# Half-width output tiles for the attention matmuls of a fused attention, spectral and gated-MLP kernel, with the key transposes moved ahead of the scores

## The chip, the core and the metric

The kernel runs on one core of one Trainium2 chip. The metric is the device time of one execution in microseconds; less is better. In the profile, PE is TensorE, PEld is its weight load (every matmul first loads its stationary operand), DVE is VectorE, ACT is ScalarE, POOL is GpSimd, and SP is the engine that issues the DMAs.

## What is computed

Three stages follow each other, in float32:

```
# 1. attention, 4 batches x 8 heads, 768 steps, head size 48
state = alpha[:, :, t, :, None] * state + einsum('bhd,bhe->bhde', k[:, :, t], v[:, :, t])
y[:, :, t] = einsum('bhd,bhde->bhe', q[:, :, t], state)
# 2. spectral mixing
theta = x @ w_theta
u = x + w_tok_r @ (x * cos(theta)) + w_tok_i @ (x * sin(theta))
x = u + relu(u @ w_ch)
# 3. gated MLP
h = relu(x @ w_in); out = (h * sigmoid(conv3(h, conv_w))) @ w_out
```

## The kernel before

Attention is done in chunks of 128 steps: 6 chunks per batch, 24 in all, numbered `ci`, with `c = ci % 6` the place in the batch. Heads go in four pairs `p` of two heads `j`; the 48 rows of a head's q and k lie at partitions 0 to 47 (j = 0) or 64 to 111 (j = 1), the partitions between them hold zeros. `a_prep` scales q and k by running products of alpha (DVE). `a_score` makes the 8 score matmuls `sc` (48 rows contracted, so two heads of a pair use different rows of the array), copies them to `pt` (ACT), masks `pt` (POOL), and then makes the 4 key transposes `kps`, copied to `kt` (ACT).

`a_y` makes the output `y` of a chunk: for each head a value matmul (stationary `pt`, 128 columns; moving `v_t`, 48 columns), and for c > 0 for each pair a state matmul (stationary q, 128 columns; moving the state `S`, 96 columns), four value and state groups one after another. ACT copies `y` to `x`. For c < 5 the state update `kv` follows: 4 matmuls (stationary `kt`, 112 columns; moving `v_t`, 96 columns), added to the state by DVE and scaled by POOL (line 293) into the other state buffer. `a_xt` transposes `x` (`xps`), `a_theta` makes `th`, and `m_mix` makes the token mixing `yps` of the batch before. All matmul operands of attention are plain float32; each such matmul stands in the trace as two records of a load and a matmul, called two passes below. The `yps`, `th`, `cps`, `hps` and `ops` matmuls use another float32 type, one pass each.

`a_att(b, c)` gives the order of the code: loads for chunk ci + 2, preparation and scores of chunk ci + 1, then `y`, state update and transposes of chunk ci. A scheduler in the framework then orders the instructions of each engine by its own estimate of times; so the order on an engine is that of the built program. PSUM tiles of attention come from one pool `ps_a` of 5 buffers; `kt` has one buffer, `pt` two.

Of the kernel before, what the change touches and what calls it, by code (L numbers as in the profile page):

```python
# [8 lines left out]
F32 = mybir.dt.float32  # L9
# [9 lines left out]
P = 128  # L19
B, H, S, D = 4, 8, 768, 48  # L20
DM = H * D
DFF = 1024
NP = H // 2
NC = S // P
# [19 lines left out]
def tile_gated_linear_attention__then__spectral_moe__then__conv_gate(  # L44
# [14 lines left out]
    nc = tc.nc  # L59
    NCH = B * NC  # L60

    def mm(o, lhsT, rhs, start, stop):
        nc.tensor.matmul(o, lhsT, rhs, start=start, stop=stop, skip_group_check=True)  # L63
# [34 lines left out]
    def body(top, slow):  # L98
# [4 lines left out]
        ident = const.tile([P, P], F32, name="ident")  # L103
# [35 lines left out]
        with ExitStack() as ph1:  # L139
# [26 lines left out]
            def apool(name, bufs, **kw):  # L166
                return att_ctx.enter_context(tc.tile_pool(name=name, bufs=bufs, **kw))
# [7 lines left out]
            ps_a = apool("ps_a", 5, space=PSUM)  # L175
# [62 lines left out]

            def a_score(ci):
                qh, kh, ftot, vt = prep[ci]  # L240
                scs = [ps_a.tile([P, NP, P], F32, tag="a", name="sc") for _ in range(2)]
                for p in range(NP):
                    for j in range(2):
                        r = slice(64 * j, 64 * j + D)
                        mm(scs[j][:, p, :], kh[r, p, :], qh[r, p, :], True, True)
                pts = []
                for j in range(2):
                    pt = att.tile([P, NP, P], F32, tag="pt", name="pt")
                    marks["pt"] = nc.scalar.copy(pt, scs[j])  # L249
                    nc.gpsimd.affine_select(pt, pt, [[0, NP], [1, P]], ALU.is_ge, 0.0, base=0, channel_multiplier=-1)  # L250
                    pts.append(pt)
                kt = None
                if ci % NC < NC - 1:
                    kps = ps_a.tile([P, 4, P], F32, tag="a", name="kps")
                    for p in range(NP):
                        nc.tensor.transpose(kps[:, p, :], kh[:, p, :], ident)  # L256
                    kt = att.tile([P, 4, P], F32, tag="kt", name="kt", bufs=1)
                    marks["kt"] = nc.scalar.copy(kt, kps)
                scored[ci] = (pts, kt)

            def a_y(ci):
                qh, kh, ftot, vt = prep.pop(ci)
                pts, kt = scored.pop(ci)
                c = ci % NC
                Sp, Sn = Sst[ci % 2], Sst[(ci + 1) % 2]
                y = ps_a.tile([P, DM], F32, tag="a", name="y")
                first = True
                for p in range(NP):
                    for j in range(2):
                        h = 2 * p + j  # L270
                        mm(y[:, h * D : (h + 1) * D], pts[j][:, p, :], vt[:, h * D : (h + 1) * D], first, c == 0)
                        first = False
                    if c > 0:
                        mm(y[:, p * 96 : p * 96 + 96], qh[:, p, :], Sp[:, p, :], False, True)
                x = x_p.tile([P, DM], F32, tag="x", name="x")
                marks["x"] = nc.scalar.copy(x, y)
                xs[ci] = x
                if c < NC - 1:
                    kv = ps_a.tile([P, NP, 2 * D], F32, tag="a", name="kv")
                    for p in range(NP):  # L280
                        mm(kv[:112, p, :], kt[:, p, :112], vt[:, p * 96 : p * 96 + 96], p == 0, True)
                    nft = prep[ci + 1][2]
                    if c > 0:
                        tt = att.tile([P, NP, 2 * D], F32, tag="tst", name="tst", bufs=1)
                        nc.vector.tensor_tensor(tt[:112], Sp[:112], kv[:112], ALU.add)
                    else:
                        tt = Sn
                        for j in range(2):
                            r = slice(64 * j, 64 * j + D)
                            nc.scalar.copy(Sn[r, :, j * D : (j + 1) * D], kv[r, :, j * D : (j + 1) * D])  # L290
                    for j in range(2):
                        r = slice(64 * j, 64 * j + D)
                        nc.gpsimd.tensor_tensor(  # L293
                            Sn[r, :, j * D : (j + 1) * D],
                            tt[r, :, j * D : (j + 1) * D],
                            nft[r].unsqueeze(2).to_broadcast([D, NP, D]),
                            ALU.mult,
                        )
# [66 lines left out]
            def a_att(b, c):  # L365
                ci = b * NC + c
                if slow:
                    xs[ci] = x_p.tile([P, DM], F32, tag="x", name="x")
                    nc.sync.dma_start(out=xs[ci], in_=x_dram[b, c * P : (c + 1) * P, :])
                    a_xt(ci)  # L370
                    return
                if ci + 2 < NCH:
                    a_load(ci + 2)
                if ci + 1 < NCH:
                    a_prep(ci + 1)
                    a_score(ci + 1)
                a_y(ci)
                a_xt(ci)

            if not slow:  # L380
                a_load(0)
                a_load(1)
                wps = ps_a.tile([P, 512], F32, tag="a", name="wps")
                for _ in range(NWARM):
                    nc.tensor.matmul(wps, onehot[:, 0, :], onehot.rearrange("p a t -> p (a t)"), start=True, stop=True)
                a_prep(0)
                a_score(0)
# [173 lines left out]
        for n, (b, h) in enumerate(units):  # L561
            if n > 0:
                m_xsplit(b, h)
            for f in range(NF):
# [3 lines left out]
                i = NF * n + f - 2 * NF  # L568
# [111 lines left out]
```

## Time and profile before

| what | value |
|---|---|
| median of 3 runs | 602.83 us (601.56 to 602.9) |
| span of the profiled execution | 604.3 us |
| PE busy in the profiled execution | 581.1 us, 96% |
| DVE, ACT, POOL busy | 457.9, 336.5, 85.2 us |
| chain that ended last: PE | 82% |

The profiled execution's own time is known as its span, from its first to its last instruction: 604.3 us, 1.5 us above the median of the timed runs; what lies around the span is not shown. Busy time counts a matmul until its last result, so that overlapping matmuls are counted once and a busy PE may still have room. The pace of a stretch is therefore read from the distance between starts of loads or matmuls.

### The profile page before, as it was taken

The page shows a single profiled execution, that of the slowest core. Times are in us where ns is not written, and L with a number is a line of the kernel's source. Part 1 is how long each engine was busy: PE and PEld are TensorE (multiplying, and loading weights), DVE is VectorE, ACT ScalarE, POOL GpSimd, SP SyncE. Part 2 cuts the span into 40 slices and gives each one's busy share as a digit, 9 for nine tenths or more (in the row PEclk, how much of TensorE's full clock was granted, in tenths as well). Part 3 has the DMA queues.
Part 4 walks back from the last instruction along what each step waited for, and adds up shares of the span by engine and source line. Part 5 has one row for each costly group of instructions (what it writes and reads, how often), then busy time and mean ns, then how long its engine had stood idle before and what let it go on. Part 6 is the DMA issues. An engine that isn't in the chain of part 4 may idle for free.

```text
span 604.3 us, 9588 instructions
## 1 busy us (share of the span) xinstructions
PE 581.1 (96%) x3703; PEld 565.9 (94%) x3703; DVE 457.9 (76%) x736; ACT 336.5 (56%) x671; POOL 85.2 (14%) x99
## 2 busy tenths in 40 slices
PE   5988999899999999999999999999999999999996
PEld 3877988899999999999999999999999999999995
DVE  7798997878945558554166888998888889888781
ACT  3464666434864347643274343656767767666571
POOL 3234413425012330133100000000000000000000
PEclk8577999969999999999999999999999999999999
DMA  8364461636003340031002333430024535446111
GB/s 313 108 213 137 134 213 56 207 116 219 19 14 91 113 160 20 14 96 50 1 1 78 105 108 108 147 112 15 26 80 128 186 118 183 149 153 197 53 41 44
DMA packets 24981, 65.33 MB, mean 108 GB/s; under 512 B 2528, under 2 KB 8672, under 8 KB 24544
## 3 DMA queue, kind: packets, MB, share of 16 engines
q1 hardware_dynamic: 24928, 64.64, 32.7%
q8 instruction: 31, 0.51, 0.3%
q14 instruction: 22, 0.18, 0.1%
HBM read 59.92 MB, written 4.72 MB: 107 GB/s over the span
## 4 chain that ended last, share of the span: by engine, by line
PE 82%; DVE 9%; ACT 3%; DMA 2%; POOL 1%; issue 1%; SPq 0%; DVEq 0%; ACTq 0%
PE yps L63 22%; PE hps L63 17%; PE ops L63 17%; PE y L63 8%; PE cps L63 6%; PE th L63 5%; PE sc L63 3%; PE kv L63 2%; DMA stage<-in_w_tok_dram 2%; DVE qk_t L236 2%; DVE fbt L225 2%; DVE fbt L230 1%; POOL S L293 1%; PE xps L309 1%; PE kps L256 1%; DVE stage L115 1%
## 5 line engine op out<-in xcount | busy, mean ns | idle before, releaser
L63 PE MATMUL yps<-wtok,zh 128*128 128x384 f32 x576 | 149.8, 342 | 0.6 <-ACT zh L71 0.6
L63 PE MATMUL hps<-x,win 128*128 128x386 f32 x576 | 107.1, 339 | 0.0
L63 PE MATMUL ops<-wout,g 128*128 128x384 f32 x576 | 106.9, 338 | 0.0
L63 PEld LDWEIGHTS yps<-wtok,zh 128*128 128x128 f32 x576 | 105.0, 191 | 0.9 <-ACT zh L71 0.7
L63 PEld LDWEIGHTS hps<-x,win 128*128 128x128 f32 x576 | 102.2, 189 | 0.0
L63 PEld LDWEIGHTS ops<-wout,g 128*128 128x128 f32 x576 | 101.8, 188 | 0.0
L63 PE MATMUL yps<-wtok,zl 128*128 128x384 f32 x288 | 97.1, 342 | 0.9 <-DVE zl L72 0.9
L250 POOL TENSOR_SCALAR_AFFINE_SELECT pt<-pt 128x512 f32<-128x512 f32 x48 | 51.5, 1095 | 180.3 <-ACT pt L249 180.2
L63 PE MATMUL y<-v_t,pt 128*128 128x48 f32 x384 | 58.8, 284 | 0.0
L225 DVE TENSOR_TENSOR_SCAN fbt<-a_t,onehot 128x512 f32<-128x512 f32 x24 | 29.9, 1246 | 35.8 <-ACT a_t L234 33.4
L63 PEld LDWEIGHTS yps<-wtok,zl 128*128 128x128 f32 x288 | 55.0, 191 | 1.6 <-DVE zl L72 1.6
L63 PEld LDWEIGHTS y<-v_t,pt 128*128 128x128 f32 x384 | 56.0, 212 | 0.5
L502 ACT ACTIVATE cv<-cv 128x384 f32<-128x384 f32 x64 | 33.4, 523 | 31.0 <-DVE cv L499 31.0
L72 DVE TENSOR_TENSOR g<-cv,g 128x384 fp32r<-128x384 f32 x64 | 35.5, 556 | 15.1 <-ACT g L71 14.5
L249 ACT COPY pt<-sc 128x512 f32<-128x512 f32 x48 | 25.7, 588 | 37.1 <-PE y L63 35.7
L63 PE MATMUL th<-wth,zh 128*128 128x384 f32 x216 | 44.4, 348 | 0.0
L496 DVE SCALAR_TENSOR_TENSOR cv<-hh,cw,cv 128x383 f32<-128x383 f32 (+1 forms) x64 | 38.4, 614 | 4.1 <-ACT cv L493 3.8
L503 DVE SCALAR_TENSOR_TENSOR cv<-cv,hh 128x384 f32<-128x384 f32 x64 | 35.2, 556 | 7.9 <-ACT cv L502 5.8
L63 PE MATMUL y<-S,qk_t 128*128 128x96 f32 x160 | 37.4, 319 | 3.1 <-POOL S L293 3.1
L63 PEld LDWEIGHTS sc<-qk_t 48*128 48x128 f32 x384 | 28.3, 200 | 12.6 <-issue 6.9
L63 PE MATMUL cps<-us,wch 128*128 128x384 f32 x216 | 40.0, 338 | 0.0
L493 ACT ACTIVATE cv<-hh,cw 128x384 f32<-128x384 f32 x64 | 38.3, 615 | 2.8 <-DVE g L72 2.5
(85 smaller groups left out, 889.5 us busy)
## 6 DMA issues: line engine op xcount, KB each, us to landing
qk_t<-in_qka_dram SPq DMA_DIRECT2D x24, 512.0 KB, 3.7
stage<-in_w_tok_dram SPq DMA_DIRECT2D x12, 768.0 KB, 4.7
top<-in_w_tok_dram SPq DMA_DIRECT2D x12, 768.0 KB, 4.4
a_t<-in_qka_dram SPq DMA_DIRECT2D x24, 260.0 KB, 2.7
v_t<-in_v_dram SPq DMA_DIRECT2D x24, 192.0 KB, 3.2
out_dram<-ob SPq DMA_DIRECT2D x24, 192.0 KB, 1.9
stage<-in_w_in_dram SPq DMA_DIRECT2D x4, 768.0 KB, 5.5
stage<-in_w_out_dram SPq DMA_DIRECT2D x4, 768.0 KB, 4.3
```

The lines of the kernel that those rows point to most:

```text
L63: nc.tensor.matmul(o, lhsT, rhs, start=start, stop=stop, skip_group_check=True)
L72: lo_eng.tensor_tensor(lo, src, hi.bitcast(F32), ALU.subtract)
L115: nc.vector.scalar_tensor_tensor(fb, hi, 0xC0000000, fb, ALU.bitwise_and, ALU.bitwise_or)
L225: nc.vector.tensor_tensor_scan(bf[:, CW - 1 :: -1], ash[:, CW - 1 :: -1], of[:, CW - 1 :: -1], 0.0, ALU.mult, ALU.add)
L230: nc.vector.tensor_tensor_scan(fo, ff, starts.rearrange("p a t -> p (a t)"), 0.0, ALU.mult, ALU.add)
L236: nc.vector.tensor_tensor(qt, qt, fl, ALU.mult)
L249: marks["pt"] = nc.scalar.copy(pt, scs[j])
L250: nc.gpsimd.affine_select(pt, pt, [[0, NP], [1, P]], ALU.is_ge, 0.0, base=0, channel_multiplier=-1)
L493: nc.scalar.activation(cv, hh[:, o : o + HALF], AF.Copy, scale=cw[:, f, 1:2])
L496: nc.vector.scalar_tensor_tensor(cv[:, a:HALF], hh[:, o + a - 1 : o + HALF - 1], cw[:, f, 0:1], cv[:, a:HALF], ALU.mult, ALU.add)
L502: nc.scalar.activation(cv, cv, AF.Tanh, scale=0.5)
L503: nc.vector.scalar_tensor_tensor(cv, cv, 1.0, hh[:, o : o + HALF], ALU.add, ALU.mult)
```

## The change

The outputs `y` and `kv` are made in two halves of 64 output rows each: the stationary operand of every value, state and update matmul is cut into two blocks of 64 columns, and each block writes to its half of the PSUM partitions (0 to 63, 64 to 127). In the built program these matmuls have a tile of 128 rows by 64 columns of the array, at column 0 or 64, instead of the full 128 by 128. The state matmuls now follow all value matmuls of a chunk. `kv` covers 128 rows instead of 112. In `a_score` the key transposes stand ahead of the scores; the copy to `kt` stays behind the copies to `pt`.

```diff
             def a_score(ci):
                 qh, kh, ftot, vt = prep[ci]
+                kt = None
+                if ci % NC < NC - 1:
+                    kps = ps_a.tile([P, 4, P], F32, tag="a", name="kps")
+                    for p in range(NP):
+                        nc.tensor.transpose(kps[:, p, :], kh[:, p, :], ident)
                 scs = [ps_a.tile([P, NP, P], F32, tag="a", name="sc") for _ in range(2)]
...
-                kt = None
                 if ci % NC < NC - 1:
-                    kps = ps_a.tile([P, 4, P], F32, tag="a", name="kps")
-                    for p in range(NP):
-                        nc.tensor.transpose(kps[:, p, :], kh[:, p, :], ident)
                     kt = att.tile([P, 4, P], F32, tag="kt", name="kt", bufs=1)
                     marks["kt"] = nc.scalar.copy(kt, kps)
...
                 y = ps_a.tile([P, DM], F32, tag="a", name="y")
-                first = True
+                halves = [slice(64 * i, 64 * i + 64) for i in range(2)]
                 for p in range(NP):
                     for j in range(2):
                         h = 2 * p + j
-                        mm(y[:, h * D : (h + 1) * D], pts[j][:, p, :], vt[:, h * D : (h + 1) * D], first, c == 0)
-                        first = False
-                    if c > 0:
-                        mm(y[:, p * 96 : p * 96 + 96], qh[:, p, :], Sp[:, p, :], False, True)
+                        for t in halves:
+                            mm(y[t, h * D : (h + 1) * D], pts[j][:, p, t], vt[:, h * D : (h + 1) * D], h == 0, c == 0)
+                if c > 0:
+                    for p in range(NP):
+                        for t in halves:
+                            mm(y[t, p * 96 : p * 96 + 96], qh[:, p, t], Sp[:, p, :], False, True)
...
                     for p in range(NP):
-                        mm(kv[:112, p, :], kt[:, p, :112], vt[:, p * 96 : p * 96 + 96], p == 0, True)
+                        for t in halves:
+                            mm(kv[t, p, :], kt[:, p, t], vt[:, p * 96 : p * 96 + 96], p == 0, True)
```

How the instructions of PE move is seen at two places of the built program. First, a chunk in the steady part, the second chunk of the third batch, before (S_112 is one of the two state buffers):

```order
L309 MATMUL xps<-ident,x 128x128 x3
L63 MATMUL sc<-qk_t 128x128 x8
L256 MATMUL kps<-ident,qk_t 128x128 x4
L63 MATMUL y<-v_t,pt 128x48 x2
L63 MATMUL y<-S_112,qk_t 128x96
L63 MATMUL y<-v_t,pt 128x48 x2
L63 MATMUL y<-S_112,qk_t 128x96
L63 MATMUL y<-v_t,pt 128x48 x2
L63 MATMUL y<-S_112,qk_t 128x96
L63 MATMUL y<-v_t,pt 128x48 x2
L63 MATMUL y<-S_112,qk_t 128x96
L63 MATMUL kv<-v_t,kt 112x96 x4
```

The same chunk on PE in the changed program:

```order
L313 MATMUL xps<-ident,x 128x128 x3
L245 MATMUL kps<-ident,qk_t 128x128 x4
L63 MATMUL sc<-qk_t 128x128 x8
L63 MATMUL y<-v_t,pt 64x48 x16
L63 MATMUL y<-S_112,qk_t 64x96 x8
L63 MATMUL kv<-v_t,kt 64x96 x8
```

The transposes stand with the full-array matmuls, the scores come next, and the value, state and update matmuls (twice as many, half as wide) follow in one block. Before, PE changed the shape of its tile twice in such a chunk (into and out of the scores); now it does so three times.

Second, PE early in the program, at the fourth chunk of the first batch, whose state matmuls wait for POOL, before:

```order
L63 MATMUL sc<-qk_t 128x128 x8
L256 MATMUL kps<-ident,qk_t 128x128 x4
L63 MATMUL y<-v_t,pt 128x48 x2
L63 MATMUL y<-S_112,qk_t 128x96
L63 MATMUL y<-v_t,pt 128x48 x2
L63 MATMUL y<-S_112,qk_t 128x96
L63 MATMUL y<-v_t,pt 128x48 x2
L63 MATMUL y<-S_112,qk_t 128x96
L63 MATMUL y<-v_t,pt 128x48 x2
L63 MATMUL y<-S_112,qk_t 128x96
L63 MATMUL yps<-wtok_84,zl 128x384
```

The same place in the changed program:

```order
L245 MATMUL kps<-ident,qk_t 128x128 x4
L63 MATMUL sc<-qk_t 128x128 x8
L63 MATMUL y<-v_t,pt 64x48 x16
L63 MATMUL y<-S_112,qk_t 64x96 x8
L63 MATMUL yps<-wtok_84,zh 128x384
```

The first state matmul stood behind two of the eight value matmuls; now it stands behind all of them.

## Rows read from the trace of the kernel before

**Rows 1.** The page: span, and granted PE clock in 40 slices, tenths.

```profile
span 604.3 us, 9588 instructions
PEclk8577999969999999999999999999999999999999
```

**Rows 2.** Busy time by stretch: stretch, length, engines' busy us (instructions), PE clock, DMA.

```profile
0.00:130.90 130.90, 113.59 (x748) 104.19 (x749) 114.23 (x160) 67.75 (x128) 45.95 (x50) 0.83 0.53 173
130.90:302.50 171.60, 171.60 (x1275) 166.44 (x1274) 100.76 (x149) 89.66 (x173) 39.10 (x48) 1.00 0.23 70
302.50:604.30 301.80, 295.91 (x1684) 295.27 (x1682) 242.89 (x427) 179.06 (x371) 0.11 (x1) 1.00 0.30 102
```

**Rows 3.** PE's matmuls by form from 130.9 to 302.5 us.

```profile
L63 PE MATMUL y<-v_t,pt 128*128 128x48 f32 x224 | 31.1, 266 | 0.0
...
L63 PE MATMUL y<-S,qk_t 128*128 128x96 f32 x96 | 20.4, 294 | 0.0
...
L63 PE MATMUL kv<-v_t,kt 128*112 128x96 f32 x88 | 10.5, 262 | 0.0
```

**Rows 4.** PE's weight loads in order of time, one steady chunk: start, us, count.

```profile
256.35 0.97 PEld L63 LDWEIGHTS sc<-qk_t 48*128 48x128 f32 x16 [0.17 <-issue]
257.44 0.42 PEld L256 LDWEIGHTS kps<-ident,qk_t 128*128 128x128 f32 x4
...
258.27 0.30 PEld L63 LDWEIGHTS y<-S,qk_t 128*128 128x128 f32 x2
258.50 0.53 PEld L63 LDWEIGHTS y<-v_t,pt 128*128 128x128 f32 x4
258.94 0.30 PEld L63 LDWEIGHTS y<-S,qk_t 128*128 128x128 f32 x2
...
260.51 0.87 PEld L63 LDWEIGHTS kv<-v_t,kt 128*112 128x112 f32 x8
261.29 0.19 PEld L63 LDWEIGHTS yps<-wtok,zh 128*128 128x128 f32 x1
```

**Rows 5.** Score loads over the whole span: duration of one in ns, min/median/max.

```profile
L63 PEld LDWEIGHTS sc<-qk_t x384: 182/188/335, 7.8 to 283.9; 48*128 48x128 f32 x192
```

**Rows 6.** Weight loads where full-array transposes meet full-array matmuls.

```profile
225.64 0.42 PEld L309 LDWEIGHTS xps<-ident,x 128*128 128x128 f32 x3
226.03 1.00 PEld L63 LDWEIGHTS th<-wth,zh 128*128 128x128 f32 x6
```

**Rows 7.** The chain that ended last, in order of time: start, us, what.

```profile
17.33 2.49 PE y L63 x12
...
47.44 4.83 POOL S L293
...
53.10 4.59 PE y L63 x20
...
121.02 4.58 PE y L63 x20
```

**Rows 8.** PE in order of time, the fourth chunk of the first batch.

```profile
53.10 0.74 PE L63 MATMUL y<-S,qk_t 128*128 128x96 f32 x2 [2.89 <-POOL S L293]
...
57.39 0.67 PE L63 MATMUL yps<-wtok,zl 128*128 128x384 f32 x1
```

**Rows 9.** Busy time by stretch, as rows 2: two stretches at the lower clock.

```profile
52.40:59.30 6.90, 6.20 (x26) 6.20 (x27) 5.59 (x10) 3.01 (x6) 1.87 (x3) 0.51 0.34 111
...
120.70:130.90 10.20, 9.94 (x42) 9.88 (x42) 9.86 (x13) 2.04 (x4) 4.58 (x5) 0.50 0.55 173
```

**Rows 10.** PE in order of time in the second of these stretches.

```profile
127.91 0.84 PE L63 MATMUL yps<-wtok,zh 128*128 128x384 f32 x2
128.55 0.52 PE L63 MATMUL yps<-wtok,zl 128*128 128x384 f32 x1
128.87 0.84 PE L63 MATMUL yps<-wtok,zh 128*128 128x384 f32 x2
```

**Rows 11.** Who waited for whom over the span: us in total, times, longest.

```profile
ACT pt L249 <- PE y L63: 35.7, 18, 5.5
```

## The prediction, made before the changed kernel was run

> **What bounds the kernel now.** I first read busy time by stretch. From 130.9 us to the end PE works with hardly a gap, at the full granted clock, while DVE is busy 100.8 of 171.6 us up to 302.5 us [rows 2]: whatever PE saves there comes straight off the time. Up to 130.9 us it is mixed: DVE is busy 114.2 of 130.9 us, PE 113.6, and the clock is at its lower level in places [rows 1, 2, 9]. There the chain of waits decides, and it goes through PE's value and state matmuls in only a few places [rows 7]. Attention ends near 302.5 us; what follows isn't touched and only moves.
>
> Next I read by form what the change touches in the PE-bound stretch: 224 passes of value matmuls, 96 of state matmuls, 88 of the update [rows 3]. That is 14 of the 24 chunks.
>
> Then the pace, from the starts of the weight loads. From one pair of state loads to the next are 0.67 us for 6 passes, 0.1117 us each, whether 48 or 96 columns stream [rows 4]. The 8 update loads, of 112 columns, take 0.78 us, 0.0975 each [rows 4]. The pace follows the columns loaded (0.00087 us per column in both), so these matmuls are bound by their loads; streaming 96 columns takes at most 0.0975.
>
> The scores show what two tiles can do: 16 loads lie within 0.97 us, and one lasts 0.188 in the median, so 8 pairs start 0.112 apart [rows 4, 5]. Both tiles of a pair load and stream together, in the time of one. But these tiles split the array's rows; no row shows a split by columns.
>
> **Cost of each part, 130.9 to 302.5 us.** Before: 320 × 0.1117 + 88 × 0.0975 = 35.7 + 8.6 = 44.3 us.
>
> The halves: passes become twice as many, at 64 columns each. A load of 64 columns, in proportion, takes 0.056 us. A pair of halves costs between 0.056 (loads and streams of both run together and loads bind) and, for 48 columns, 0.112, for 96 columns twice the streaming of one (both halves one after another). I take the lower kind, since it is nearest to the only two-tile row, the scores. For 48 moving columns that is 0.056. For 96 columns streaming may bind: the scores stream 128 columns in at most 0.112, so 96 in about 0.084; bounds 0.056 and 0.0975. After: 224 pairs × 0.056 + (96 + 88) pairs × 0.084 = 12.5 + 15.5 = 28.0 us. Saved: 16.3 us. That `kv` now has 128 rows instead of 112 is in this.
>
> The third change of tile shape: at the entry to the scores the loads stand idle 0.17 us; at their exit the last pair starts at about 257.13, the next load would come at 257.24 and comes at 257.44, so 0.20 [rows 4]. Between matmuls of one shape there is no such gap [rows 6]. I take 0.18 for a change into or out of column halves, which no row shows; below, nothing, and above, twice that. 14 chunks × 0.18 = +2.5 us. Had the transposes stayed behind the scores, it would be one change more; their move costs PE nothing.
>
> What the moved transposes delay: scores start one block of transposes (about 0.45 us) later. Behind them on ACT are the copies to `pt`, which wait anyway for the value matmuls of the chunk before to let go of `pt` (35.7 us in all, 18 times) [rows 11]; and those now end earlier, since the state matmuls no longer stand between them. The transposes' PSUM buffer is now the first of the ring, so `xps` waits for the copy to `kt`, which waits for `kv`. In the steady part the yps passes between `kv` and `xps` (16 in the new order, about 0.16 each, half the cold 0.32 [rows 10]) cover it with 2.6 us. In the first batch nothing does, and it can cost up to about one copy, 0.6 us, a chunk. No DMA is added or moved past a wait.
>
> **Up to 130.9 us.** At two places of the chain the state matmul waits for POOL, and 20 passes follow it at the lower clock: 53.10 to 57.39, 4.29 us, 0.214 a pass, and the like at 121.02 [rows 7, 8]. After the change the value matmuls are done during the wait, and only 8 pairs of state passes follow, at twice 0.084: 1.3 us. That is 3.0 us off, twice. The 12 value passes at 17.33 (2.49 us) become 12 pairs at 0.112, 1.3 off [rows 7]. Together 7.3 us, less about four colder shape changes at 0.36, 1.4: some 6 us if nothing else takes over. DVE is 87% busy there [rows 2], so I keep half: 3 us, with 0 and 6 as bounds.
>
> **Sum.** −16.3 + 2.5 − 3 = −16.8 us, all of it from the profiled execution, whose span is 604.3; the median of the runs is 0.2% lower, too little to change these differences. So 602.8 − 16.8 = 586.0 us. Its own range: 96-column pairs at 0.056 give 5.2 less and the early part up to 3 less, 578; 96-column pairs at 0.0975 (+2.5), shape changes at twice the price (+2.5) and no early gain (+3) give 594.
>
> The Trainium skill ("TensorE: Matmul & The Clock Gate", Part 3, "Measured speedup vs the span model") gives 2.38 times for three column tiles, 0.79 of the ideal; taken over to two tiles, an estimate, 56.0 us of halves one after another would take 35.2 instead of 28.0, and the time would be 593. No row here shows it.
>
> **Rivals.**
>
> *One: a pair of halves goes no faster than a pair of scores*, 0.112 us, because four instructions of a pair (two loads, two matmuls) come no faster than there. For it: no row shows them faster. Against it: the scores' pace is that of a 128-column load, which explains it already. Then 408 pairs × 0.1117 = 45.6, +1.3; shape changes +2.5; early, 8 cold pairs at 0.214 still replace 20 passes, −2.6 twice, less 1.4, half kept: −2. Time 604.6: no gain.
>
> *Two, on the other side: the halves run one after another*, because both use all rows of the array and loads or streams of one wait for the other. The value passes then cost 448 × 0.056 = 25.1, state and update (192 + 176) × 0.084 = 30.9; 56.0 against 44.3 is +11.7; shape changes +2.5; early gains about 0. Time 617. It decides as soon as a pair takes over 0.11 us on average (44.3 − 2.5 + 3 = 44.8 us over 408 pairs). For it: in the scores the two tiles share no rows, here they share all.
>
> The Trainium skill ("TensorE: Matmul & The Clock Gate", Part 3, "The mechanism") says that a load overlaps matmuls in flight only where the row groups differ; the halves have the same ones, so by it this rival or worse would come. The trace does not agree with it as it stands: value loads of the full array start every 0.112 us while each such matmul lasts 0.266 on the same rows [rows 3, 4]. It adds something to this rival's chance, not all.
>
> *Three: the clock.* PE gets less to do between 59.3 and 120.7 us, where it waits at times, and another stretch such as 120.7 to 130.9 falls at the lower clock [rows 9]. A yps pass takes 0.32 there [rows 10] and half of that otherwise; 10.2 us would lose at most 5.1. Time 591 to 594.
>
> **Chances.** Forecast 0.60; clock 0.08; rival one 0.17; rival two 0.15. The range of 8 in 10 leaves out rival two and the tails: 578 to 606; the likeliest case alone, 578 to 594. A measurement of this kernel tells 0.3%, 1.8 us, from no change. Forecast and clock are faster by more; of rival one I give 0.03 to faster, 0.07 to within, 0.07 to slower. Faster 0.71, same 0.07, slower 0.22.
>
> **What the profile after would show.** Records of `y` and `kv` doubled to 1088 and 320. Right, if in a steady chunk 32 loads of `y` from value matmuls lie within about 1 us, in pairs some 0.056 apart, 16 state and 16 update loads in about 0.7 each, and the steady stretch is some 14 us shorter with PE still full. One gap of about 0.18 between scores and values, one behind `kv`. Early, a POOL wait followed by some 1.3 us of state passes instead of 4.3. Wrong, if loads of the two halves follow each other without overlap (rival two), pairs stand at 0.11 (rival one), gaps at the new shape are far above 0.18, `xps` waits for ACT in the steady part, or the granted clock falls between 59 and 120 us.

## The result, and the profile after

The changed kernel takes 583.11 us in the median of 4 runs (582.55 to 583.78) against 602.19 for the kernel before; the ratio is 0.969, with a 95% interval from 0.9666 to 0.9714. The forecast was 586.0 us, between 578 and 606, and faster with a chance of 0.71.

The page of the changed kernel, its span, busy times and granted clock:

```profile
span 581.8 us, 10995 instructions
PE 550.6 (95%) x4407; PEld 531.5 (91%) x4407; DVE 463.1 (80%) x736; ACT 337.0 (58%) x671; POOL 95.6 (16%) x99
PEclk9589898999999999999999999999999999999999
```

PE has 704 records more and 30 us less busy time. These are the weight loads of one steady chunk, in order of time (start, us, count):

```profile
175.13 0.47 PEld L245 LDWEIGHTS kps<-ident,qk_t 128*128 128x128 f32 x4
175.77 0.97 PEld L63 LDWEIGHTS sc<-qk_t 48*128 48x128 f32 x16 [0.17 <-issue]
176.86 1.01 PEld L63 LDWEIGHTS y<-v_t,pt 128*64 128x64 f32 x32
177.79 0.70 PEld L63 LDWEIGHTS y<-S,qk_t 128*64 128x64 f32 x16
178.43 0.72 PEld L63 LDWEIGHTS kv<-v_t,kt 128*64 128x64 f32 x16
179.27 0.30 PEld L63 LDWEIGHTS yps<-wtok,zh 128*128 128x128 f32 x2
```

This answers to [rows 4]. 32 value loads begin within 0.93 us, until the state loads begin: 16 pairs at 0.058 us. Loads of one half alone start 0.058 us apart too (the halves apart, below), so 32 one after another would need 1.86 us: two run at a time. 8 pairs of state loads take 0.64 us, 0.080 each; the last `kv` load starts 0.72 − 0.137 behind the first, 7 steps of 0.083. The stationary operand's 64 columns bind the values, the 96 streamed columns bind state and update, as the sum had it (0.056 and 0.084); the quarters below bear this out. The new change of shape is seen behind `kv`: its last load starts at 179.01, the next would come at 179.10 and comes at 179.27, 0.17 us.

The groups of `y` and `kv` over the whole span (min/median/max ns of one):

```profile
L63 PEld LDWEIGHTS y<-v_t,pt x768: 132/138/230, 15.3 to 268.6; 128*64 128x64 f32 x192
L63 PE MATMUL y<-v_t,pt x768: 222/222/340, 15.3 to 268.7; 128*64 128x48 f32 x192
L63 PEld LDWEIGHTS y<-S,qk_t x320: 133/137/230, 26.1 to 269.3; 128*64 128x64 f32 x160
...
  ACT pt L254: 15.9, 17
```

```profile
L63 PEld LDWEIGHTS kv<-v_t,kt x320: 132/137/230, 15.5 to 264.2; 128*64 128x64 f32 x160
```

The records are doubled as forecast, 768 + 320 and 320. ACT's wait for `y` before it may write `pt` again, 35.7 us in [rows 11], is 15.9: the values now end before the state matmuls.

To compare stretches I cut each trace where the twelfth chunk's `xps` begins and where the first `cps` begins. The changed kernel (length, busy us, clock, DMA):

```profile
0.00:140.03 140.03, 113.59 (x1244) 101.26 (x1244) 130.55 (x179) 77.26 (x146) 57.64 (x56) 0.90 0.57 185
140.03:323.27 183.24, 183.24 (x1729) 177.67 (x1727) 119.64 (x178) 102.32 (x196) 38.00 (x43) 1.00 0.20 63
323.27:581.80 258.53, 253.73 (x1438) 252.57 (x1437) 212.92 (x381) 157.47 (x330) 0.00 (x0) 1.00 0.32 108
```

The kernel before, cut at the same places:

```profile
0.00:150.38 150.38, 133.07 (x902) 123.00 (x903) 129.87 (x181) 77.21 (x146) 53.90 (x56) 0.85 0.53 172
150.38:345.06 194.68, 194.68 (x1366) 190.19 (x1365) 114.89 (x175) 101.64 (x195) 31.27 (x43) 1.00 0.19 59
345.06:604.30 259.24, 253.35 (x1438) 252.71 (x1437) 213.13 (x382) 157.62 (x330) 0.00 (x0) 1.00 0.32 108
```

The steady stretch of 12 chunks is 11.4 us shorter, with PE full in both. The early stretch is 10.4 us shorter, and in it DVE is now busy 130.6 of 140.0 us while PE has 26 us to spare. The rest is the same within 0.7 us. The work on either side of the first cut is not quite the same: by the starts of their loads, 197 `yps` passes lie ahead of it before and 187 in the changed kernel, 600 and 610 between the cuts. So 10 passes, 1.7 us at the steady pace of 0.174, moved from the stretch where PE has room into the one where it is full.

The spans differ by 22.5 us, the runs by 19.1: the profiled execution of before was a long one, which an experiment below shows. In every run for which both are known the time is 1.7 to 2.0 us above the span, so that execution took about 606 us, some 4 more than the median of the runs.

### The profile page after: what moved, and what is told of

Read it like the earlier page. It is cut to its first block, busy times and chain, and to the rows that moved or that the text cites. A ratio compares the mean times of both kernels' runs of the same rounds, so it can differ in the third digit from the quotient of the medians.

```text
span 581.8 us, 10995 instructions
## 1 busy us (share of the span) xinstructions
PE 550.6 (95%) x4407; PEld 531.5 (91%) x4407; DVE 463.1 (80%) x736; ACT 337.0 (58%) x671; POOL 95.6 (16%) x99
## 4 chain that ended last, share of the span: by engine, by line
PE 80%; DVE 16%; issue 2%; ACT 1%; DMA 0%; DVEq 0%; ACTq 0%
PE yps L63 22%; PE hps L63 17%; PE ops L63 17%; PE cps L63 7%; PE th L63 5%; PE y L63 5%; PE sc L63 3%; DVE qk_t L236 3%; DVE fbt L225 2%; DVE fbt L230 2%; DVE stage L115 2%; PE kv L63 2%; DVE wtok L72 1%; DVE stage L116 1%; PE xps L313 1%
## 5 line engine op out<-in xcount | busy, mean ns | idle before, releaser
L63 PE MATMUL yps<-wtok,zh 128*128 128x384 f32 x576 | 151.7, 343 | 0.0
L63 PE MATMUL yps<-wtok,zl 128*128 128x384 f32 x288 | 95.3, 337 | 0.5 <-DVE zl L72 0.5
L255 POOL TENSOR_SCALAR_AFFINE_SELECT pt<-pt 128x512 f32<-128x512 f32 x48 | 56.5, 1197 | 129.4 <-ACT pt L254 129.1
L225 DVE TENSOR_TENSOR_SCAN fbt<-a_t,onehot 128x512 f32<-128x512 f32 x24 | 31.3, 1305 | 24.2 <-ACT a_t L234 21.9
L71 ACT CAST g<-cv 128x384 fp32r<-128x384 f32 x64 | 32.6, 509 | 11.6 <-DVE cv L507 10.1
L63 PEld LDWEIGHTS th<-wth,zh 128*128 128x128 f32 x216 | 38.8, 194 | 0.1
L503 DVE SCALAR_TENSOR_TENSOR cv<-hh,cw,cv 128x384 f32<-128x384 f32 (+1 forms) x64 | 38.3, 612 | 0.7
L314 ACT COPY u<-xps 128x384 f32<-128x384 f32 x24 | 11.5, 480 | 47.0 <-PE xps L313 47.0
L63 PEld LDWEIGHTS cps<-us,wch 128*128 128x128 f32 x216 | 38.0, 188 | 0.5 <-issue 0.3
```

The lines of the kernel that those rows point to most:

```text
L71: cast = nc.scalar.copy(hi, src)
L225: nc.vector.tensor_tensor_scan(bf[:, CW - 1 :: -1], ash[:, CW - 1 :: -1], of[:, CW - 1 :: -1], 0.0, ALU.mult, ALU.add)
L503: nc.vector.scalar_tensor_tensor(cv[:, 0:e], hh[:, o + 1 : o + 1 + e], cw[:, f, 2:3], cv[:, 0:e], ALU.mult, ALU.add)
```

## The experiments

Each ratio is to the kernel before on the same chip, with its 95% interval; its medians there are 601.9 to 603.0 us, so medians from different chips can be compared to about 1 us.

| kernel | median us | ratio (interval) |
|---|---|---|
| full tiles, new order | 598.99 | 0.9961 (0.9941 to 0.9981) |
| transposes behind the scores | 585.06 | 0.973 (0.970 to 0.976) |
| halves apart | 596.32 | 0.9916 (0.9888 to 0.9944) |
| quarters | 587.39 | 0.9749 (0.9717 to 0.9781) |
| before, profiled again | 602.11 | one run |
| values alone in halves | 588.87 | 0.979 (0.9739 to 0.9842) |
| changed, less DVE work | 577.10 | 0.9578 (0.9537 to 0.9618) |
| before, less DVE work | 598.98 | 0.9951 (0.9908 to 0.9994) |
| low parts on POOL | 594.96 | 0.9863 (0.9811 to 0.9914) |
| products on POOL | 590.27 | 0.9799 (0.9742 to 0.9857) |
| changed, again | 583.01 | 0.9677 (0.9626 to 0.9728) |

**Full tiles in the new order.** My theory was that the halves gain because two load and stream together; the first rival, that the new order alone gains.

```diff
-                halves = [slice(64 * i, 64 * i + 64) for i in range(2)]
+                halves = [slice(0, P)]
...
-                        for t in halves:
-                            mm(kv[t, p, :], kt[:, p, t], vt[:, p * 96 : p * 96 + 96], p == 0, True)
+                        mm(kv[:112, p, :], kt[:, p, :112], vt[:, p * 96 : p * 96 + 96], p == 0, True)
```

> Full tiles again (128 output rows of y, 112 of kv), but with the transposes ahead of the scores and all state matmuls behind all value matmuls, as in the changed kernel. Theory A (the gain is the two column halves that load and stream together): the stretch from the last attention transpose of the second batch to the first cps matmul is again within 1.5 us of the 194.7 us of before (183.2 in the changed kernel), and the whole keeps only the early gain of the moved state matmuls, 2 to 7 us of the 19: 595 to 600 us. Rival B (the new order is what gains, not the halves): 583 to 588 us, and the stretch near 183.

Measured: 598.99 us, 0.4% less than before. Its stretches:

```profile
0.00:141.28 141.28, 126.16 (x890) 115.36 (x891) 129.41 (x180) 77.46 (x146) 52.21 (x56) 0.90 0.56 183
141.28:336.94 195.66, 195.66 (x1382) 191.97 (x1381) 118.60 (x177) 103.50 (x196) 34.67 (x43) 1.00 0.19 59
```

The steady stretch is 195.66 us long, 1.0 more than with the old order, and holds 615 `yps` passes instead of 600, some 2.6 us. From load to load, its value, state and update passes take 38.2 us in it, as before (38.4), against 24.2 with the halves and 2.0 for the change of shape behind them; so the gain in these passes is the halves' alone. The early stretch, however, is 141.28 us, nearly as short as with the halves. The halves are worth 599.0 − 583.1 = 15.9 us, the order about 2.4 in the runs (4.4 in the spans profiled, 600.2 of the second profile of before against 595.8; the execution profiled here took 1.5 us less than the median of its ten runs).

**Transposes behind the scores.** What does one change of tile shape more cost?

```diff
-                if ci % NC < NC - 1:
-                    kps = ps_a.tile([P, 4, P], F32, tag="a", name="kps")
-                    for p in range(NP):
-                        nc.tensor.transpose(kps[:, p, :], kh[:, p, :], ident)
                 scs = [ps_a.tile([P, NP, P], F32, tag="a", name="sc") for _ in range(2)]
...
                 if ci % NC < NC - 1:
+                    kps = ps_a.tile([P, 4, P], F32, tag="a", name="kps")
+                    for p in range(NP):
+                        nc.tensor.transpose(kps[:, p, :], kh[:, p, :], ident)
```

> The changed kernel with the transposes behind the scores, as before: one more change of tile shape a chunk (scores to full array, full array to halves, instead of scores to halves). Theory A: a change costs about 0.18 us, so the 12 chunks of the steady stretch take about 1.8 us more (10 of them have transposes) and the early part, where DVE is busy 130.6 of 140 us, hides its share: 584 to 587 us. Rival B: a change that involves halves costs nothing or is hidden: 583 us within 0.3%. Rival C: it costs twice as much or more: 588 us and over.

Measured: 585.06 us. The weight loads of a steady chunk:

```profile
173.92 0.97 PEld L63 LDWEIGHTS sc<-qk_t 48*128 48x128 f32 x16 [0.17 <-issue]
175.01 0.42 PEld L256 LDWEIGHTS kps<-ident,qk_t 128*128 128x128 f32 x4
175.59 1.01 PEld L63 LDWEIGHTS y<-v_t,pt 128*64 128x64 f32 x32 [0.17 <-issue]
```

There is a second idle of 0.17 us ahead of the values, where full array turns into halves. The steady stretch (138.12 to 322.84, 184.7 us) is 1.5 us longer than the changed kernel's, for a forecast of 1.8. In the runs it is 2 us; the two intervals of the ratios touch, so the size rests on the trace.

**Halves apart.** The same half-width matmuls, but not neighbours.

```diff
-                for p in range(NP):
-                    for j in range(2):
-                        h = 2 * p + j
-                        for t in halves:
+                for t in halves:
+                    for p in range(NP):
+                        for j in range(2):
+                            h = 2 * p + j
...
-                    for p in range(NP):
-                        for t in halves:
+                    for t in halves:
+                        for p in range(NP):
```

> The changed kernel with the same half-width matmuls, but all of the lower half of y first and then all of the upper, and the same for the state matmuls and kv: no two neighbours use different halves. Theory A (the gain is the overlap of neighbours): loads follow each other at 0.058 us for y and 0.085 for state and kv, a steady chunk takes 32 x 0.058 + 32 x 0.085 = 4.6 us instead of 2.3, 12 chunks 27 us more, so at least 605 us and up to 625. Rival B (PE pairs passes over a distance, or narrower loads alone gain): within 5 us of 583.

Measured: 596.32 us, 13.2 more than with neighbouring halves, so most of the gain is in the pairing; but 605 was the least expected. The steady stretch is 195.6 us long, as with full tiles. The weight loads of a chunk:

```profile
179.59 1.57 PEld L63 LDWEIGHTS y<-v_t,pt 128*64 128x64 f32 x29
181.08 0.13 PEld L63 LDWEIGHTS y<-S,qk_t 128*64 128x64 f32 x1
181.09 0.14 PEld L63 LDWEIGHTS y<-v_t,pt 128*64 128x64 f32 x1
...
181.21 0.77 PEld L63 LDWEIGHTS y<-S,qk_t 128*64 128x64 f32 x12
...
182.07 0.85 PEld L63 LDWEIGHTS kv<-v_t,kt 128*64 128x64 f32 x13
183.04 0.19 PEld L63 LDWEIGHTS yps<-wtok,zh 128*128 128x128 f32 x1
```

From the first value load to the load behind `kv` it takes 3.45 us, against 2.41 in the changed kernel (176.86 to 179.27); 12 chunks make 12.5 us. One after another they would take 32 × 0.056 + 32 × 0.084 + 0.17 = 4.65 by the prediction's prices of one. State loads begin while value loads still come, and update loads while state loads still come: PE runs the first passes of one block beside the last of the other half's block. Two or three loads of a block share the time of the last ones of the block before. My expectation had no overlap at all. Where a half is alone, its loads start as far apart as pairs of neighbouring halves do, (0.55 − 0.138) / 7 = 0.059 us:

```profile
179.82 0.55 PEld L63 LDWEIGHTS y<-v_t,pt 128*64 128x64 f32 x8
```

**Quarters.** If a group of tiles costs the longer of one load and one stream, four tiles of 32 make the values cheaper still.

```diff
-                halves = [slice(64 * i, 64 * i + 64) for i in range(2)]
+                halves = [slice(32 * i, 32 * i + 32) for i in range(4)]
```

> The changed kernel with four column tiles of 32 output rows instead of two of 64, for y, state and kv. Theory A (a group costs the longer of one tile's load and one tile's stream): value groups fall from 0.058 to about 0.042 us (48 columns streamed at the pace of the state's 96 in 0.085), 0.26 us a chunk; state and kv stay at 0.085 since streaming binds; 12 steady chunks 3 us less, the early part bound by DVE: 579 to 582 us. Rival B (loads and matmuls come no faster than 0.0145 us each, the pace of the value pairs now): eight of them take 0.116, a chunk takes 3.7 us instead of 2.3, 12 chunks 17 us more: 595 to 605 us.

Measured: 587.39 us, slower than halves. The loads of a steady chunk:

```profile
184.50 0.75 PEld L63 LDWEIGHTS y<-v_t,pt 128*32 128x32 f32 x64
185.17 0.67 PEld L63 LDWEIGHTS y<-S,qk_t 128*32 128x32 f32 x32
185.79 0.71 PEld L63 LDWEIGHTS kv<-v_t,kt 128*32 128x32 f32 x32
```

The price came as theory A says: 64 value loads in 0.67 us, 16 groups at 0.042, and state and update as before. The time did not. Its stretches:

```profile
0.00:140.23 140.23, 109.34 (x1933) 94.60 (x1933) 129.57 (x180) 76.72 (x145) 63.27 (x56) 0.90 0.57 185
140.23:326.00 185.77, 183.95 (x2447) 176.82 (x2446) 117.00 (x175) 103.69 (x196) 35.42 (x43) 1.00 0.21 63
326.00:586.20 260.20, 253.96 (x1438) 252.55 (x1437) 213.60 (x382) 157.61 (x330) 0.00 (x0) 1.00 0.32 107
```

The early part is as long as with the halves, DVE being as busy in it, and PE does less in it (109.3 us busy against 113.6): the steady stretch has 626 `yps` matmuls instead of 611, at 0.174 us some 2.6 us of work that this kernel's order put off. PE also waits 1.8 us in that stretch. Together this is 1.4 us more than the 3 us saved; the stretch is 2.5 us longer, and the rest of that isn't traced here; 1.7 us in the last stretch, where the work is the same, I can't name. So rival one of the prediction is refuted at its root (eight instructions of a group in 0.042 us), and yet a cheaper pass gave a slower kernel.

**The kernel before, profiled again.** Nothing is changed.

> The kernel before, unchanged, profiled once more. Theory A (the execution profiled first was a long one, held up by a stretch at the lower clock near 120 us): the span is near 600 us, less than 604.3, and the granted clock does not stand at the lower level for 10 us between 118 and 132 us; the end of attention comes some 3 us earlier. Rival B (every execution is like the one profiled): span 604 us and the same stretch.

Measured: a span of 600.2 us. Its stretches:

```profile
0.00:147.02 147.02, 131.40 (x901) 119.92 (x902) 129.37 (x181) 77.08 (x146) 51.46 (x56) 0.87 0.54 176
147.02:341.71 194.69, 194.69 (x1367) 190.20 (x1365) 115.24 (x176) 101.69 (x196) 31.26 (x43) 1.00 0.19 59
118.00:131.00 13.00, 11.39 (x100) 10.49 (x97) 12.72 (x18) 6.49 (x12) 5.17 (x6) 1.00 0.63 215
```

The steady stretch is the same to 0.01 us; the early one is 3.4 shorter, and between 118 and 131 us the full clock was granted, where [rows 9] has half of it for 10.2 us. The first profile is not the only such execution: of the 34 runs of the kernel before beside the experiments, those with a mean granted clock of 0.966 or more took 599.8 to 603.1 us, the four at 0.960 or less 605.3 to 607.3. Against this execution the change gives −7.0 us early, −11.45 in the steady stretch and nothing after it, 18.4 in all, which fits the runs.

**Values alone in halves.** State matmuls with 128 and update with 112 columns, otherwise as changed.

```diff
-                        for t in halves:
-                            mm(y[t, p * 96 : p * 96 + 96], qh[:, p, t], Sp[:, p, :], False, True)
+                        mm(y[:, p * 96 : p * 96 + 96], qh[:, p, :], Sp[:, p, :], False, True)
...
-                            mm(kv[t, p, :], kt[:, p, t], vt[:, p * 96 : p * 96 + 96], p == 0, True)
+                        mm(kv[:112, p, :], kt[:, p, :112], vt[:, p * 96 : p * 96 + 96], p == 0, True)
```

> The changed kernel with halves for the value matmuls alone; state matmuls with 128 columns and kv with 112 as before, in the new order. Theory A (a pair of halves costs the longer of half a load and one stream, so the values, where half a load binds, carry most): per steady chunk state 0.89 instead of 0.68 us and kv 0.78 instead of 0.67, 0.3 us a chunk, 12 chunks 3.5 us more than the changed kernel, the early part bound by DVE: 585 to 588 us. Rival B (state and kv carry as much as the values): 590 us and over.

Measured: 588.87 us, a little above the 585 to 588 expected, with a wide interval. In the trace the steady stretch (139.75 to 326.64, 186.89 us) is 3.65 us longer than the changed kernel's, for 3.5 expected; the span is 4.3 longer, the medians differ by 5.8. So in the steady stretch the values carry some 8 of the 11.4 us; where the rest of the difference between the runs comes from stays open.

**Less DVE work, in both kernels.** The third decoding instruction is left out for the token weights alone, which leaves out their lowest three bits.

```diff
-        def decode(full, st, n):
+        def decode(full, st, n, low=True):
...
-            nc.vector.scalar_tensor_tensor(fb, lo, 29, fb, ALU.logical_shift_right, ALU.bitwise_or)
+            if low:
+                nc.vector.scalar_tensor_tensor(fb, lo, 29, fb, ALU.logical_shift_right, ALU.bitwise_or)
...
-            decode(full, st, n)
+            decode(full, st, n, tag != "st" or scale is not None)
```

> The changed kernel without the third of the three DVE instructions that decode a block of token weights, 12 instructions of about 0.95 us on DVE less in the first 140 us (it leaves out the lowest three bits of these weights). Theory A (since the change DVE alone sets the length of the first 140 us): the time falls by 7 to 11 us, to 572 to 577. Rival B (PE and waits still set it): by less than 4 us.

> The kernel before without the same 12 DVE instructions (it leaves out the lowest three bits of the token weights). Theory A (before the change PE shared the chain of the first 150 us with DVE): the time falls, but by less than the changed kernel's does, 3 to 7 us, to 595 to 599. Rival B (DVE set that stretch already before): it falls by 7 to 11 us, as in the changed kernel, and the early gain of the change was not one of PE's share.

Measured: the changed kernel falls to 577.10, by 6.0 us, and just misses its 7 to 11; the kernel before falls to 598.98, by some 3 to 4. The ten runs of the latter lie between 596.3 and 605.1, and the interval of its ratio, 0.9908 to 0.9994, means a gain of 0.4 to 5.5 us; so the runs alone hardly part the two falls. The traces say more. The changed kernel's early stretch without these instructions:

```profile
0.00:132.09 132.09, 112.79 (x1243) 99.21 (x1244) 119.71 (x167) 76.79 (x146) 51.85 (x56) 0.92 0.60 196
```

It is 7.9 us shorter for 10.8 us less on DVE, and DVE is still busy 91% of it. The same stretch of the kernel before without them:

```profile
0.00:148.02 148.02, 135.17 (x901) 125.39 (x902) 119.70 (x169) 77.34 (x146) 46.66 (x56) 0.84 0.53 175
```

With 10 us less on DVE it lies between the two with these instructions (147.02 and 150.38), in one execution, with a mean clock of 0.84 against 0.87 and 0.85. The order fits theory A, DVE bounding the early part more since the change; its busy share there, 93% against 86 to 88%, says the same.

**Two tries to relieve DVE.** Work of DVE is given to POOL, which has room: the low parts of the token weights, or the products of x with sine and cosine.

```diff
-            cast = split(out_hi, out_lo, full, nc.vector)
+            cast = split(out_hi, out_lo, full, nc.gpsimd if tag == "st" and scale is None and not slow else nc.vector)
```

> The changed kernel with the low parts of the token weights (11 subtractions of 768 elements, 1.03 us each on DVE in the first 140 us) made by POOL, which is busy 57.6 of 140 us there. Theory A (DVE alone bounds the first 140 us and POOL has room): 4 to 8 us less than the changed kernel, 575 to 579 us. Rival B (POOL's queue then delays the masks of pt and the scaling of the state, on which the state matmuls wait): no gain or a loss, 582 us and over.

```diff
-                nc.vector.tensor_tensor(z, x.unsqueeze(1).to_broadcast([P, 2, DM]), z, ALU.mult)
+                nc.gpsimd.tensor_tensor(z, x.unsqueeze(1).to_broadcast([P, 2, DM]), z, ALU.mult)
```

> The changed kernel with the products of x with sine and cosine (24 over the kernel, 6 in the first 140 us, 1.02 us each on DVE there) made by POOL. Theory A (DVE bounds the first 140 us): 2 to 5 us less than the changed kernel, 578 to 581 us. Rival B (POOL takes longer for each and is on the way from th to the token mixing, or slows DVE): no gain or a loss, 582 us and over.

Measured: 594.96 and 590.27 us; both lose, 12 and 7 us. In the first, up to 150 us, by group:

```profile
L72 POOL TENSOR_TENSOR wtok<-stage,wtok 128x768 fp32r<-128x768 f32 x11 | 23.3, 2120 | 11.0 <-ACT wtok L71 10.4
...
L225 DVE TENSOR_TENSOR_SCAN fbt<-a_t,onehot 128x512 f32<-128x512 f32 x14 | 24.4, 1744 | 6.4 <-ACT a_t L234 4.5 <-DMA a_t<-in_qka_dram 1.8
```

The same groups in the changed kernel, up to 140 us:

```profile
L225 DVE TENSOR_TENSOR_SCAN fbt<-a_t,onehot 128x512 f32<-128x512 f32 x14 | 19.1, 1363 | 2.3 <-DMA a_t<-in_qka_dram 1.9
L72 DVE TENSOR_TENSOR wtok<-stage,wtok 128x768 fp32r<-128x768 f32 x11 | 11.3, 1027 | 1.2 <-ACT wtok L71 1.2
```

A subtraction takes 2.12 us on POOL, 1.03 on DVE; and the 14 scans of line 225 on DVE, 1.36 us in the mean of the changed kernel, take 1.74 here. DVE got less work and grew slower: it is busy 134.6 us up to 150 us, against 130.6 up to 140.0 with the subtractions on it. In the second try a product takes 2.47 us on POOL, 1.02 on DVE; the scans stay at 1.34 us, but the first two decoding instructions take 0.95 and 1.27 us in the mean instead of 0.69 and 1.04. How much of either loss is DVE's slower work, and how much POOL's slower work on the way of the weights and products, no run separates.

**The changed kernel again**, beside these two:

> The changed kernel once more, beside the two others on the same chip. Theory A (nothing but the run differs): 581 to 585 us and the first 140 us as before, since DVE sets them. Rival B (its early part varies from execution to execution as that of the kernel before does, by 3 us and more): attention's 12th transposes away from 140.0 us by over 2 us.

Measured: 583.01 us, a span of 581.3, the twelfth `xps` at 139.3 us instead of 140.0: it repeats, as theory A says.

## Why the prediction was right, step by step

1. *Halves of a pair load and stream together.* Right. Forecast 0.056 and 0.084 us a pair, seen 0.058 and 0.080 to 0.083. By the prediction's own terms the 12 chunks of the steady stretch go from 30.4 + 7.8 = 38.2 to 24.2 us, plus 12 × 0.18 = 2.2: −11.8. From load to load, with the changes of shape behind them, these passes took 38.4 us before and 26.2 after, −12.2. That the whole stretch is shorter by nearly the same, 11.4, is in part luck: 10 more `yps` passes lie in it (+1.7), and PE enters the scores 11 times instead of 13, since the order of before had the scores of two chunks in two parts (two entries at 0.26 and two exits at 0.20 us, −0.9). Full tiles gain nothing in these passes, and halves apart lose the gain of the stretch.
2. *The third change of shape, 0.18 us.* Right: 0.17 behind `kv`, 0.17 ahead of the values when the transposes stand between.
3. *The early part, 3 us with 0 and 6 as bounds.* This is the step that failed in size. Two of the 14 chunks that I counted as steady fall in the part that DVE bounds, so the prediction has −2.0 − 3 = −5.0 there; measured against the second profile of before, −7.0, with 10 `yps` passes fewer in it. The forecast was 2.9 us too high: 0.6 because the kernel before, 602.83 in three runs, is 602.19 in four; the other 2.3 because the gain was 19.1 and not 16.8, and these 2.0 are most of that. That the sum came so near is in part luck, for its working had a term that was an accident of one execution: the lower clock at 121 us, which made 20 passes cost 4.6 us there, isn't there in the second profile. Nor could the values have been done during the wait at that place, for PE had waited only 0.26 us there for POOL:

```profile
121.02 0.74 PE L63 MATMUL y<-S,qk_t 128*128 128x96 f32 x2 [0.26 <-POOL S L293]
```

The 12 passes at 17.33 would give 2.49 − 12 × 0.112 = 1.15 us, not 1.3. And what gains early is above all the order: full tiles in the new order reach the same place 5.7 us earlier in their profile, the halves 1.3 more. The place can be seen in the changed kernel, PE in order of time at the fourth chunk, for [rows 8]:

```profile
46.58 1.14 PE L63 MATMUL y<-v_t,pt 128*64 128x48 f32 x32
49.34 0.88 PE L63 MATMUL y<-S,qk_t 128*64 128x96 f32 x16 [1.63 <-POOL S L297]
50.16 1.32 PE L63 MATMUL yps<-wtok,zh 128*128 128x384 f32 x6
```

Behind POOL's wait come 0.82 us of state passes instead of 4.29, as forecast in kind; the clock was at full level here, so it is less than the 1.3 forecast.

4. *DVE would take over part of the early gain.* Right in kind: DVE is busy 130.6 of 140.0 us, and less work on it takes 6.0 us off the changed kernel and 3 to 4 off the one before, a difference that fits but that the runs hardly show by themselves.
5. *`xps` in the first batch may wait for ACT.* It does, but not for the copy to `kt` that the prediction named: the four waits are for the copy of `y` to `x`, which `xps` reads, three of them in the first batch and none in the steady part. PE's waits in the changed kernel:

```profile
PE xps L313 <- ACT x L279: 8.4, 4, 4.3
PE kps L245 <- DVE qk_t L236: 6.5, 4, 2.7
```

The first was 4.4 us in four waits before. The chain that ended last goes through two of them, at 20.7 and 33.3 us, and from there to 132 us mostly through DVE.

6. *Rivals.* One (a pair at the pace of the scores) is refuted by the pairs at 0.058 and the groups of four at 0.042. Two (halves one after another) is what the halves apart show in large part, and it cost 13 us; as priced, 617, it would have needed no overlap anywhere. Three (the clock) came in kind, though not in price: the lower level was granted between 59 and 120 us, which the prediction had named as a sign of being wrong, from 63.8 to 67.3 and from 91.2 to 94.6 us. PE had waited 3.2 us for POOL until 63.15, and 1.3 us for DVE until 90.82. Inside these stretches:

```profile
64.00:67.00 3.00, 3.00 (x23) 2.78 (x20) 3.00 (x6) 0.99 (x2) 1.11 (x1) 0.50 0.61 171
91.50:94.00 2.50, 2.50 (x14) 2.28 (x11) 2.50 (x3) 2.50 (x7) 1.91 (x2) 0.50 0.28 77
```

DVE is busy all through both. Over the whole early stretch the mean clock is 0.90, against 0.85 and 0.87 before, from which some 28 us at the lower level can be worked out, against 45 and 38; and the stretch at 120.7, on which this rival was priced, was an accident.

The rule that spoke against the change does not hold here: the Trainium skill ("TensorE: Matmul & The Clock Gate", Part 3, "The mechanism") lets a load overlap matmuls in flight only where row groups differ, and here both halves use all rows, a matmul of the values lasts 0.222 us, and a pair of loads starts every 0.058. Its 2.38 for three column tiles with 512 streamed columns ("Measured speedup vs the span model"), 0.79 of the ideal, is less than two reach here: one half alone starts a load every 0.058 or 0.059 us, neighbouring halves a pair every 0.058, so two value tiles do twice the work of one in the same time.

## What to carry to other kernels

Where matmuls are short against their weight loads, read the pace from the starts of the loads: if it follows the loaded columns, two column tiles in neighbouring instructions may halve it, as here, until one tile's streaming binds; each change of tile shape cost about 0.17 us here, so group by shape. Put what waits (here the state matmuls) behind everything that doesn't. When two kernels are compared by stretches, count what lies in each, since a new order moves work across the cuts. And before pricing a gain in a mixed stretch, profile it twice: a stretch at the lower clock may be of that execution alone, and the next engine (here DVE) takes what is saved.

## What the runs showed that was not expected

PE runs half tiles beside each other over a short distance in the program too: with all of one half ahead of the other, a chunk took 3.45 us, not 4.65. Passes of a quarter tile start 16 groups of four in 0.67 us, and the kernel is still slower, in part since the schedule that comes with them puts PE's other work off. With subtractions moved from DVE to POOL, DVE's scans took 1.74 us in the mean instead of 1.36; with the products moved, they did not grow, and decoding instructions did. The Trainium skill ("SBUF — State Buffer", "Who interferes with whom") has DVE instructions with two SBUF inputs and GpSimd ones that read SBUF exclude each other on a shared port; the scan has two such inputs, and the first try agrees with it, though no run here separates it from other causes.
